# A planned attention-and-MLP kernel: gelu in runs of six, wv loaded among the first x tiles, the last output block in one bank

## The chip, the cores and the metric

The kernel runs on one core of a Trainium2 chip. The metric is device time in microseconds (us). The engines are TensorE (PE in the profile, PEld for its weight loads), VectorE (DVE), ScalarE (ACT), GpSimd (POOL) and SyncE (SP), which here issues every DMA. Each engine runs its own instruction list in order and waits on semaphores for the others.

## What is computed

With x of 2048 rows by 1024, 32 heads of 32, and a hidden width of 3584, all in bf16:

```python
xn = layernorm(x)
s = softmax(q k^T / sqrt(32)) v @ wo            # q, k, v from xn @ wqkv, 32 heads
y = layernorm(xn)
g = silu(gelu(y @ w1 + b1) @ w2 + b2)           # gelu in its tanh form
out = x + s * g
```

## The kernel before

**Tiling.** Attention works in 8 head groups of 4 heads and 8 blocks of 256 queries. A *unit* is one block of queries against 256 keys for the 4 heads of a group: PE computes the scores (line 902, eight matmuls of 256 columns) into two pairs of PSUM banks out of three pairs, ACT takes the exponential of each pair (line 911, 128x1024, two for a unit), and PE multiplies the result with V (line 625). There are 64 units of scores for each head group, so close to a thousand exponentials. VectorE adds the exponentials up for the softmax sums (lines 928 and 942). The MLP works in 8 chunks of 256 rows. A chunk has 14 `w1_item`s; each makes two blocks of 128 hidden units by 256 rows in one bank (line 630) and adds the bias on VectorE into a slot of the ring `hT` of 20 slots (line 1084). Gelu is applied to a *run* of slots that lie side by side: three VectorE instructions (lines 1098 to 1100) prepare the argument in a scratch tile `ut`, ACT takes Tanh (line 1101), and two more VectorE instructions (1102, 1103) finish it in `hT`. Runs have 4 slots (2048 elements a partition) or 2 slots (1024), and use the two `ut` tiles in turn. Then 4 `w2_item`s make the chunk's output (line 630 again), with a Tanh of 1024 elements for the silu (line 1128), and the result goes to DRAM (`g_scratch`). The last head group also does the product with wo and the final `x + s * g` (lines 1428 to 1458).

**The order of the work.** No loop order is fixed by hand. Every instruction is added to a planner (`_Plan`) with its engine, an estimated duration, a priority and the tokens it reads and writes. `run` lays the instructions out in time on all five engines and so decides each engine's order; `settle` turns the dependencies into semaphore waits. PE takes scores first when their inputs are there, then a V group, then "dense" groups (projections, MLP, output) in the order of a position and a due time, each in bank 6 or 7. An instruction once placed waits in its place at run time, and everything behind it on that engine waits too. Durations in the planner steer the order and nothing else.

**The start.** SP issues the loads of x tiles 0 to 3, the first K and Q weights, and x tiles 4 to 11 (`load_x`, line 639). A tile is normalized on VectorE (statistics line 837, result line 796 into `gw`). Tiles 0 to 3 and 5 are transposed on PE (line 780) and copied out by ACT (line 784); the others go through a DMA transpose into `xnT` (line 800, queue of SP). x tiles 12 to 15 and, after tile 13, the first V weights `wv` (line 653) are loaded with a wait for the normalization of tile 4. K of a pair of tiles is projected by `k_item(n)`, its bank copied to SBUF by ACT (line 754) for n below 3 and by VectorE (line 751) from 3 on; Q's bank is copied by VectorE (line 738). The first V groups are `v_half` (line 630, matmuls `ps<-wv,xnT` of 128 columns). Where PE has nothing to do early on, the planner puts in small matmuls on the identity (line 680).

**The end.** The last 256 rows of the output are four blocks of 128x512 (i2 = 0 to 3). For each, the product with wo over head chunks 0 to 6 is finished early in a bank `most`, read by VectorE into an f32 tile (1439) and added to x (1442). The last head chunk, whose input is ready last, goes to another bank (2 to 5); VectorE multiplies it (1452; for block 3 ACT reads the bank, 1447, and VectorE multiplies, 1449), adds the f32 tile (1455, f32 operand) and SP stores the block (1458). The stores carry the tokens `rt` of their row tile, so that the second store of a row tile waits for the first to land.

Of the kernel before, what the change touches and what calls it, by code (L numbers as in the profile page):

```python
# [6 lines left out]
ACT = mybir.ActivationFunctionType  # L7
# [460 lines left out]
def bass_recurrent_scan__mha_block__mixer_channel_mlp__prompt_kernel(  # L468
# [31 lines left out]
    with ExitStack() as st:  # L500
        def sb(name, shape, dt):
            return st.enter_context(nc.sbuf_tensor(name, list(shape), dt))
# [5 lines left out]
        TRP = (5,)  # L508
        PN = ()
        NTR, NWARM, NG0, AT = 4, 8, 3, (1, 3)  # L510
        ident = sb("ident", [128, 128], BF16)
# [16 lines left out]
        b1T = sb("b1T", [128, FB], BF16)  # L528
        ut_t = [sb(f"ut{i}", [128, 4, 512], BF16) for i in range(2)]
        gw = sb("gw", [128, 4096], BF16)  # L530
# [29 lines left out]
        xnb = [gw[:, i * 1024:(i + 1) * 1024] for i in range(4)]  # L560
        iota_i = ut_t[0][:].rearrange("p a b -> p (a b)")[:, 0:256].bitcast(I32)

# [49 lines left out]
        def pool(fn, occ, R, W, prio=3):  # L612
            return add("POOL", fn, occ, PL, R, W, prio)
# [128 lines left out]
        def k_item(n):  # L742
            it = _Item("pro", 0.01 * n)
            for lo, w in ((0, 128), (128, 128)) if n < 2 else ((0, 256),):
                for dc in range(DC):
                    def fn(e, b, dc=dc, lo=lo, w=w):
                        at = n * 256 + lo
                        return mm(e, bank(b, lo, lo + w), wqk[wk0][:, dc, :], xnT[:, dc, at:at + w], dc == 0 and lo == 0, dc == DC - 1)
                    chunk(it, fn, Q256 if w == 256 else Q128, [("xnT", 2 * n + i, dc) for i in range(lo // 128, (lo + w) // 128)] + [("wqk", wk0)])
            if n >= 3:  # L750
                dve(lambda e: e.tensor_copy(QKT[0][:, 1, n * 256:(n + 1) * 256], bank(it.bank, 0, 256)), c_ps(256), [],
                    [("K", 0, n)], -1, it)
                return it
            act(lambda e: e.activation(QKT[0][:, 1, n * 256:(n + 1) * 256], bank(it.bank, 0, 256), ACT.Copy), c_act(256), [],
                [("K", 0, n)], -1, it)
            return it
# [37 lines left out]
        def normalize(t, rs):  # L794
            def nf(e):
                return e.tensor_scalar(xnb[t % 4], xst[t], mv[:, t, 0:1], lnp[:, t, 1:2], op0=ALU.subtract, op1=ALU.mult)  # L796
            rw = ([XS(t), ("mv", t), rs], [("xnb", t % 4)], 1)
            first[t] = pool(nf, 1150, *rw) if t in PN else dve(nf, c_b4(1024) + 118, *rw)
            if t >= NTR and t not in TRP:
                dma(f"tr{t}", lambda e: e.dma_start_transpose(xnT[:, :, t * 128:(t + 1) * 128], xnb[t % 4]), 262144,  # L800
                    [("xnb", t % 4)], [("xnT", t, c) for c in range(DC)], prio=0, rate=300.0, occ=1300, lat={4: 2800, 6: 2400, 7: 2000}.get(t, 1000))

# [260 lines left out]
        def make_y(c):  # L1063
            for t2 in range(2):
# [7 lines left out]
                    262144, [("yst", t2)], [("yT", t2)], occ=1300, rate=300.0, lat=2300)  # L1072

        def w1_item(c, pi):
            p = c * NW1 + pi
            gi, hs = p % NW1R, p % NH
            it = _Item("mlp")
            for f2 in range(2):
# [7 lines left out]
                c_ps(512), [("b1",)], [("h", hs)], 0, it)  # L1086
            half = c == NCH - 1 and pi in (NW1 - 3, NW1 - 1)
            if p % 4 != 3 and pi != NW1 - 1 and not (pi == 1 and c % 2) and not half:
                return it
            k = 2 if (pi == NW1 - 1 and p % 4 != 3) or (pi == 1 and c % 2) or half else 4  # L1090
            h0, n = hs - k + 1, k * 512
            hs_ = [("h", h0 + i) for i in range(k)]
            ui = geg["n"] % 2
            geg["n"] += 1
            x_ = hT[:, h0:h0 + k].rearrange("p s k t -> p (s k t)")
            u_ = ut_t[ui][:].rearrange("p a b -> p (a b)")[:, 0:n]
            gp, ga = (1.4, -1) if c == NCH - 1 and pi >= 5 else (3, 1)
            dve(lambda e: e.tensor_tensor(u_, x_, x_, op=ALU.mult), c_b16(n), hs_, [("ut", ui)], gp)  # L1098
            dve(lambda e: e.tensor_scalar(u_, u_, GA, 1.0, op0=ALU.mult, op1=ALU.add), c_b4(n), [("ut", ui)], [("ut", ui)], gp)
            dve(lambda e: e.tensor_tensor(u_, u_, x_, op=ALU.mult), c_b16(n), [("ut", ui)] + hs_, [("ut", ui)], gp)  # L1100
            act(lambda e: e.activation(u_, u_, ACT.Tanh, scale=GC), c_acts(n), [("ut", ui)], [("ut", ui)], ga)  # L1101
            dve(lambda e: e.tensor_scalar_add(u_, u_, 1.0), c_b4(n), [("ut", ui)], [("ut", ui)], gp)
            dve(lambda e: e.tensor_tensor(x_, u_, x_, op=ALU.mult), c_b16(n), [("ut", ui)] + hs_, hs_, gp)  # L1103
            return it
# [213 lines left out]
        for w in range(HG):  # L1318
# [24 lines left out]
            for qb in range(NQB):  # L1343
# [44 lines left out]
                for t2 in range(2):  # L1388
# [16 lines left out]
                    for nh in range(2):  # L1405
# [3 lines left out]
                        i2 = 2 * t2 + nh  # L1409
                        sl_ = slice(nh * 512, (nh + 1) * 512)  # L1410
                        if late:
                            most = _Item("wo", it.pos + 64)
                            plan.dense["last"].append(most)
                            if fin:
                                it.bank = 2 + 2 * t2 + nh
                                if not t2:
                                    it.due = 64 * HG - 2
                            (plan.dense["wo"] if not fin else lates if t2 else firsts).append(it)
                        for hc in range(HG):
                            def fn(e, b, hc=hc, tb=tb, nh=nh, late=late):  # L1420
                                return mm(e, bank(b), OTr[:, hc, tb * 128:tb * 128 + 128],
                                          wo_at[hc][:, nh * 512:(nh + 1) * 512], hc == 0 or late and hc == HG - 1,
                                          hc == HG - 1 or late and hc == HG - 2)
                            chunk(most if late and hc < HG - 1 else it, fn, Q512,
                                  [("OTr", hc) if hc < 7 else ("OTr", 7, qb) + ((t2,) if fin else ()), ("wo", hc)],
                                  [("S", 1 + t2, nh)] if fin and hc == HG - 1 else ())
                        if not late:
# [9 lines left out]
                        if not fin:  # L1437
                            after([("xf", xk)], [("w1", i) for i in range(NW1R)])
                        dve(lambda e, most=most, gr=gr, sl_=sl_, xf=xf: e.scalar_tensor_tensor(
                            xf, bank(most.bank), 0.5, gr[:, sl_], op0=ALU.mult, op1=ALU.mult),  # L1440
                            c_ps(512), [("gr", ri, nh)], [("xf", xk)] + (zs if fin else []), 0, most)
                        dve(lambda e, xr=xr, sl_=sl_, xf=xf: e.tensor_tensor(xf, xf, xr[:, sl_], op=ALU.add),
                            c_f32(512), [("xr", ri, nh)], [("xf", xk)], 2)
                        if fin and i2 == 3:
# [6 lines left out]
                        else:  # L1451
                            dve(lambda e, it=it, gr=gr, sl_=sl_: e.scalar_tensor_tensor(gr[:, sl_], bank(it.bank), 0.5,
                                                                                        gr[:, sl_], op0=ALU.mult, op1=ALU.mult),
                                c_ps(512), [], [("gr", ri, nh)], -1 if fin and t2 else 0, it)
                        dve(lambda e, xr=xr, gr=gr, sl_=sl_, xf=xf: e.tensor_tensor(xr[:, sl_], gr[:, sl_], xf, op=ALU.add),
                            c_f32(512), [("gr", ri, nh), ("xf", xk)], [("xr", ri, nh)], -1 + 0.1 * i2 if fin and t2 else 2.05 if fin else 1)
                        if fin:
                          dma(f"osl{i2}", lambda e, xr=xr, tb=tb, sl_=sl_: e.dma_start(
                            out2[tb * 128:(tb + 1) * 128, sl_], xr[:, sl_]), 131072, [("xr", ri, nh)], rt, prio=0, rate=390.0, lat=1000.0)
                    if fin:  # L1460
# [69 lines left out]
```

## Time and profile before

| what | value |
|---|---|
| timed runs | 1032.63, 1033.36, 1033.86 us; median 1033.36 |
| the profiled execution | 1032.24 us; its span, from first to last instruction, 1030.3 us |
| busy ACT | 1016.9 us (99%), of it 988 exponentials from line 911 into the tiles P: 922.4 us |
| busy PE, DVE, POOL | 1004.7, 956.3, 11.8 us |
| granted TensorE clock, mean | 0.997 of full speed |

Busy time is the time in which at least one instruction of the engine was running, as the profiler shows it; ends of matmuls are modelled, so PE's figure is not a measure of work at peak. An instruction's duration holds a part in which the next one has already begun, so the distance from start to start is what an instruction costs on a full engine; the chain of waits lists such distances, and the groups list durations.

### The profile page before, as it was taken

The page shows a single profiled execution, that of the slowest core. Times are in us where ns is not written, and L with a number is a line of the kernel's source. Part 1 is how long each engine was busy: PE and PEld are TensorE (multiplying, and loading weights), DVE is VectorE, ACT ScalarE, POOL GpSimd, SP SyncE. Part 2 cuts the span into 40 slices and gives each one's busy share as a digit, 9 for nine tenths or more (in the row PEclk, how much of TensorE's full clock was granted, in tenths as well). Part 3 has the DMA queues.
Part 4 walks back from the last instruction along what each step waited for, and adds up shares of the span by engine and source line. Part 5 has one row for each costly group of instructions (what it writes and reads, how often), then busy time and mean ns, then how long its engine had stood idle before and what let it go on. Part 6 is the DMA issues. An engine that isn't in the chain of part 4 may idle for free.

```text
span 1030.3 us, 31971 instructions
## 1 busy us (share of the span) xinstructions
PE 1004.7 (98%) x14355; PEld 636.6 (62%) x14355; DVE 956.3 (93%) x1347; ACT 1016.9 (99%) x1093; POOL 11.8 (1%) x21
## 2 busy tenths in 40 slices
PE   8999999999999999999999999999999999999996
PEld 6666656666666567566665676666666665654443
DVE  8899999899899999997899989998999889978987
ACT  8999999999999999999999999999999999999996
POOL 2200000000000000000000000000000000000000
PEclk9999999999999999999999999999999999999999
DMA  8867746645765658456547576565455752974321
GB/s 222 158 156 206 200 136 182 170 117 142 204 175 154 182 157 228 125 144 188 139 126 195 143 215 173 158 177 152 118 154 167 216 168 78 279 224 124 112 91 58
DMA packets 317144, 167.75 MB, mean 163 GB/s; under 512 B 55632, under 2 KB 304976, under 8 KB 317008
## 3 DMA queue, kind: packets, MB, share of 16 engines
q1 hardware_dynamic: 317008, 165.71, 58.8%
q8 instruction: 112, 1.84, 0.7%
q14 instruction: 24, 0.20, 0.1%
HBM read 146.55 MB, written 12.06 MB: 154 GB/s over the span
## 4 chain that ended last, share of the span: by engine, by line
ACT 84%; PE 7%; DVE 5%; DMA 2%; issue 0%; SPq 0%; POOL 0%; DVEq 0%
ACT P L911 78%; PE ps L630 4%; ACT ut L1101 4%; PE ps L625 2%; ACT gw L1128 1%; PE ps L902 1%; ACT P L1221 1%; DVE PA L928 1%; DMA wv<-in_A_wqkv_dram 1%; DVE stats L837 1%; DVE PR L942 1%; DVE hT L1084 1%; DMA yst<-in_A_x_dram 1%; DVE gw L796 0%; DMA hT<-in_A_x_dram 0%; DMA xnT<-gw 0%
## 5 line engine op out<-in xcount | busy, mean ns | idle before, releaser
L911 ACT ACTIVATE P<-ps 128x1024 bf16<-128x1024 f32 x988 | 922.4, 1231 | 0.6 <-PE ps L902 0.5
L928 DVE TENSOR_TENSOR PA<-P 128x2048 bf16<-128x2048 bf16 x173 | 209.8, 1215 | 30.0 <-ACT P L911 29.5
L630 PE MATMUL ps<-yT,w1r 128*128 128x256 bf16 x1792 | 228.0, 273 | 0.9 <-DVE V L716 0.4
L630 PE MATMUL ps<-w2r,hT 128*128 128x256 bf16 x1792 | 224.3, 273 | 0.7 <-DVE nt L997 0.3
L942 DVE TENSOR_TENSOR PR<-PR,PA 128x2048 bf16<-128x2048 bf16 x173 | 209.1, 1210 | 1.2
L902 PE MATMUL ps<-QKT 32*128 32x256 bf16 x4032 | 200.4, 273 | 9.2 <-ACT P L911 7.0
L630 PEld LDWEIGHTS ps<-yT,w1r 128*128 128x128 bf16 x1792 | 164.5, 98 | 53.5 <-issue 28.1
L630 PEld LDWEIGHTS ps<-w2r,hT 128*128 128x128 bf16 x1792 | 163.0, 98 | 51.5 <-issue 31.3
L902 PEld LDWEIGHTS ps<-QKT 32*128 32x128 bf16 x4032 | 59.8, 92 | 137.3 <-ACT P L911 129.4
L625 PE MATMUL ps<-P,V 128*32 128x256 bf16 (+1 forms) x4080 | 137.2, 272 | 0.2
L630 PE MATMUL ps<-xnT,wqk 128*128 128x512 bf16 (+2 forms) x584 | 131.3, 354 | 1.1 <-DVE nv L1010 0.3
L625 PEld LDWEIGHTS ps<-P,V 128*32 128x32 bf16 x4080 | 95.6, 96 | 32.7 <-issue 22.6
L630 PE MATMUL ps<-wv,xnT 128*128 128x256 bf16 (+2 forms) x704 | 89.7, 267 | 1.6 <-DMA xnT<-gw 0.6
L630 PEld LDWEIGHTS ps<-xnT,wqk 128*128 128x128 bf16 x584 | 50.0, 98 | 50.7 <-issue 14.4
L1084 DVE TENSOR_TENSOR hT<-ps,b1T 128x512 bf16<-128x512 f32 x112 | 76.6, 684 | 3.7 <-PE ps L630 3.2
L928 DVE TENSOR_TENSOR PR<-P 128x2048 bf16<-128x2048 bf16 x60 | 72.7, 1212 | 0.1
L630 PEld LDWEIGHTS ps<-wv,xnT 128*128 128x128 bf16 x704 | 56.5, 99 | 25.6 <-issue 11.6
L1101 ACT ACTIVATE ut<-ut 128x2048 bf16<-128x2048 bf16 (+1 forms) x33 | 61.4, 1861 | 0.0
L728 DVE CAST QKT<-ps 128x512 bf16<-128x512 f32 x58 | 39.6, 683 | 1.6 <-PE ps L630 1.2
L997 DVE STREAM_TRANSPOSE nt<-ps 128x256 f32<-128x256 f32 x63 | 27.9, 442 | 13.8 <-PE ps L625 13.4
L1103 DVE TENSOR_TENSOR hT<-ut,hT 128x2048 bf16<-128x2048 bf16 (+1 forms) x33 | 34.6, 1049 | 0.1
L1098 DVE TENSOR_TENSOR ut<-hT 128x2048 bf16<-128x2048 bf16 (+1 forms) x33 | 34.7, 1050 | 0.1
(115 smaller groups left out, 584.9 us busy)
## 6 DMA issues: line engine op xcount, KB each, us to landing
w1r<-in_B_w_dram SPq DMA_DIRECT2D x112, 512.0 KB, 4.7
w2r<-in_B_w_dram SPq DMA_DIRECT2D x128, 448.0 KB, 4.5
yst<-in_A_x_dram SPq DMA_DIRECT2D x18, 256.0 KB, 4.7
wqk<-in_A_wqkv_dram SPq DMA_DIRECT2D x16, 256.0 KB, 3.7
g_scratch<-gw SPq DMA_DIRECT2D x32, 128.0 KB, 2.9
hT<-in_A_x_dram SPq DMA_DIRECT2D x14, 256.0 KB, 3.9
o_scratch<-ot SPq DMA_DIRECT2D x56, 64.0 KB, 3.6
xnT<-o_scratch SPq DMA_DIRECT2D x7, 512.0 KB, 5.3
```

Source lines behind the costliest of these rows:

```text
L625: ins = e.matmul(dst(j), lhsT=lhsT(j), rhs=rhs(j), start=start, stop=stop, tile_position=(0, 32 * j), skip_group_check=True)
L630: return e.matmul(dst, lhsT=lhsT, rhs=rhs, start=start, stop=stop, skip_group_check=True)
L728: dve(lambda e: e.tensor_copy(QKT[sl][:, which, tq * 512:(tq + 1) * 512], bank(it.bank)), c_ps(512), [], [(nm, sl, 2 * tq), (nm, sl, 2 * t ...
L902: ins = e.matmul(bank(b0[j], kk * 256, (kk + 1) * 256), lhsT=QKT[sl][32 * j:32 * j + 32, 1, kb * 128:(kb + 1) * 128], rhs=QKT[sl][32 * j:3 ...
L911: x = act(lambda e, h=h: e.activation(Pt[pi][:, 2 * h:2 * h + 2].rearrange("p j k q -> p (j k q)"), ps[:, pr[h] * 1024:(pr[h] + 1) * 1024] ...
L928: return dve(lambda e: e.tensor_tensor(dst[:].rearrange("p u j q -> p (u j) q"), src[:].rearrange("p u j k q -> p (u j) k q")[:, :, 0, :], ...
L942: return dve(lambda e: e.tensor_tensor(fl3(pr), fl3(pr), fl3(PA[i]), op=ALU.add), c_b16(2048), [("PA", i), tok], [tok], 3.2)
L997: dve(lambda e: e.transpose(nt_t[:], bank(pv.bank, 256, 512)), c_ps(256) + 120, [], [("nt",)], prio, pv)
L1084: w1_ev[p] = dve(lambda e: e.tensor_tensor(hT[:, hs], bank(it.bank).rearrange("p (k t) -> p k t", k=2), b1T[:, 2 * pi:2 * pi + 2].unsqueez ...
L1098: dve(lambda e: e.tensor_tensor(u_, x_, x_, op=ALU.mult), c_b16(n), hs_, [("ut", ui)], gp)
L1101: act(lambda e: e.activation(u_, u_, ACT.Tanh, scale=GC), c_acts(n), [("ut", ui)], [("ut", ui)], ga)
L1103: dve(lambda e: e.tensor_tensor(x_, u_, x_, op=ALU.mult), c_b16(n), [("ut", ui)] + hs_, hs_, gp)
```

## The change

Five things change.

1. **Gelu runs.** A table `GRUNS` is made before the MLP: in chunks 0 to 5 a run has up to 6 slots (`GMAX`), in the last two up to 4, never across the end of the ring of 20; in the last chunk it ends in runs of 2. A run of 6 uses both `ut` tiles, now one tensor `utw`, with VectorE's five instructions done in two parts (4 slots and 2 slots) and one Tanh over 3072 elements. The number of runs goes from 33 to 27.
2. **wv and x12 to x15.** `load_v(0)` stands between x9 and x10, with no wait. x12 and x13 are added with a wait for the normalization of tile 4 before pair 3, x14 and x15 with a wait for that of tile 7 before pair 4.
3. **K copy of pair 2** goes from ACT (line 754) to VectorE: `n >= 2`.
4. **The last output block** (i2 = 3) is `whole`: head chunks 0 to 7 add up in one bank, so the f32 copy and its addition (1439, 1442) fall away for this block, ACT still reads the bank, and the last addition has bf16 operands. It stands alone in a queue `pre`.
5. **The final stores** no longer carry `rt`. Some latencies that the planner assumes for DMA transposes change.

```diff
-        for t in range(NTR, 12):
-            load_x(t)
+        load_x(4)
...
+        load_x(9)
+        load_v(0)
+        load_x(10)
+        load_x(11)
...
-            if n >= 3:
+            if n >= 2:
                 dve(lambda e: e.tensor_copy(QKT[0][:, 1, n * 256:(n + 1) * 256], bank(it.bank, 0, 256)), c_ps(256), [],
...
-            if n == 6:
-                for t in range(12, NT):
-                    load_x(t, [first[4]])
-                    if t == 13:
-                        load_v(0, [first[4]])
+            if n == 3:
+                load_x(12, [first[4]])
+                load_x(13, [first[4]])
+            if n == 4:
+                load_x(14, [first[7]])
+                load_x(15, [first[7]])
...
+        GRUNS = {}
+        for c_ in range(NCH):
+            p_, end = c_ * NW1, (c_ + 1) * NW1
+            while p_ < end:
+                k_ = min(GMAX if c_ < 6 else 4, end - p_, NH - p_ % NH)
+                if c_ == NCH - 1:
+                    k_ = min(k_, 2 if end - p_ <= 4 else 4)
+                GRUNS[p_ + k_ - 1] = k_
+                p_ += k_
...
-            act(lambda e: e.activation(u_, u_, ACT.Tanh, scale=GC), c_acts(n), [("ut", ui)], [("ut", ui)], ga)
...
+            for h0, k, ui in parts:
...
+                dve(lambda e, u_=u_, x_=x_: e.tensor_tensor(u_, x_, x_, op=ALU.mult), c_b16(n), hs_, [("ut", ui)], gp)
+                dve(lambda e, u_=u_: e.tensor_scalar(u_, u_, GA, 1.0, op0=ALU.mult, op1=ALU.add), c_b4(n), [("ut", ui)], [("ut", ui)], gp)
+                dve(lambda e, u_=u_, x_=x_: e.tensor_tensor(u_, u_, x_, op=ALU.mult), c_b16(n), [("ut", ui)] + hs_, [("ut", ui)], gp)
...
+            act(lambda e: e.activation(ua, ua, ACT.Tanh, scale=GC), c_acts(run * 512), uts, uts, ga)
...
+                        whole = fin and i2 == 3
...
-                        dve(lambda e, most=most, gr=gr, sl_=sl_, xf=xf: e.scalar_tensor_tensor(
-                            xf, bank(most.bank), 0.5, gr[:, sl_], op0=ALU.mult, op1=ALU.mult),
-                            c_ps(512), [("gr", ri, nh)], [("xf", xk)] + (zs if fin else []), 0, most)
-                        dve(lambda e, xr=xr, sl_=sl_, xf=xf: e.tensor_tensor(xf, xf, xr[:, sl_], op=ALU.add),
-                            c_f32(512), [("xr", ri, nh)], [("xf", xk)], 2)
+                        if not whole:
...
+                        if whole:
+                            dve(lambda e, xr=xr, gr=gr, sl_=sl_: e.tensor_tensor(xr[:, sl_], gr[:, sl_], xr[:, sl_], op=ALU.add),
+                                c_b16(512), [("gr", ri, nh)], [("xr", ri, nh)], -1 + 0.1 * i2)
...
-                            out2[tb * 128:(tb + 1) * 128, sl_], xr[:, sl_]), 131072, [("xr", ri, nh)], rt, prio=0, rate=390.0, lat=1000.0)
+                            out2[tb * 128:(tb + 1) * 128, sl_], xr[:, sl_]), 131072, [("xr", ri, nh)], [], prio=0, rate=390.0, lat=1000.0)
```

More of the change, by code (lines that the diff above doesn't have):

```diff
@@ L509, in bass_recurrent_scan__mha_block__mixer_channel_mlp__prompt_kernel @@
         PN = ()
+        GMAX = 6
         NTR, NWARM, NG0, AT = 4, 8, 3, (1, 3)
@@ L1102, in w1_item @@
-            dve(lambda e: e.tensor_scalar_add(u_, u_, 1.0), c_b4(n), [("ut", ui)], [("ut", ui)], gp)
-            dve(lambda e: e.tensor_tensor(x_, u_, x_, op=ALU.mult), c_b16(n), [("ut", ui)] + hs_, hs_, gp)
+            run = GRUNS.get(p)
+            if run is None:
+                return it
+            hh = hs - run + 1
+            gp, ga = (1.4, -1) if c == NCH - 1 and pi >= 5 else (3, 1)
+            parts = []
+            for h0 in range(hh, hh + run, 4):
+                k = min(4, hh + run - h0)
+                ui = 0 if h0 > hh or run > 4 else geg["n"] % 2
+                parts.append([h0, k, ui])
@@ new lines, in w1_item @@
+            if run > 4:
+                parts[1][2] = 1
+                geg["n"] = 0
+            else:
+                geg["n"] += 1
+            views = []
+            for h0, k, ui in parts:
+                hs_ = [("h", h0 + i) for i in range(k)]
+                n = k * 512
+                x_ = hT[:, h0:h0 + k].rearrange("p s k t -> p (s k t)")
+                u_ = utw[:, 4 * ui:4 * ui + k].rearrange("p a b -> p (a b)")
+                views.append((x_, u_, n, hs_, ui))
+                dve(lambda e, u_=u_, x_=x_: e.tensor_tensor(u_, x_, x_, op=ALU.mult), c_b16(n), hs_, [("ut", ui)], gp)
+                dve(lambda e, u_=u_: e.tensor_scalar(u_, u_, GA, 1.0, op0=ALU.mult, op1=ALU.add), c_b4(n), [("ut", ui)], [("ut", ui)], gp)
+                dve(lambda e, u_=u_, x_=x_: e.tensor_tensor(u_, u_, x_, op=ALU.mult), c_b16(n), [("ut", ui)] + hs_, [("ut", ui)], gp)
@@ new lines, in w1_item @@
+            u0 = 4 * parts[0][2]
+            ua = utw[:, u0:u0 + run].rearrange("p a b -> p (a b)")
+            uts = [("ut", q_[2]) for q_ in parts]
+            act(lambda e: e.activation(ua, ua, ACT.Tanh, scale=GC), c_acts(run * 512), uts, uts, ga)
+            for x_, u_, n, hs_, ui in views:
+                dve(lambda e, u_=u_: e.tensor_scalar_add(u_, u_, 1.0), c_b4(n), [("ut", ui)], [("ut", ui)], gp)
+                dve(lambda e, u_=u_, x_=x_: e.tensor_tensor(x_, u_, x_, op=ALU.mult), c_b16(n), [("ut", ui)] + hs_, hs_, gp)
```

53 lines of the change are left out of this document (28 added, 25 removed).

## The prediction

> **What bounds the kernel now.** I read the page's busy times and chain of waits first, then ACT alone in order of time, since it is the fullest engine.
>
> ```profile
> PE 1004.7 (98%) x14355; PEld 636.6 (62%) x14355; DVE 956.3 (93%) x1347; ACT 1016.9 (99%) x1093; POOL 11.8 (1%) x21
> ...
> ACT 84%; PE 7%; DVE 5%; DMA 2%; issue 0%; SPq 0%; POOL 0%; DVEq 0%
> ```
>
> ACT is busy 1016.9 of 1030.3 us. Its idle time is only 13.4 us, and the busy times by stretch place it: 3.36 us in 0 to 20 us, 1.81 in 20 to 40, 0.42 in 40 to 60, 0.03 in 60 to 1000, and 7.76 in the last 30.3, where after the last exponential (1021.94) the other engines finish alone. So a change gains three ways only: less work on ACT, less idle ACT at the start, a shorter end. Anything on PE, DVE or DMA in between is worth nothing unless it makes ACT wait.
>
> ACT at the start, in order of time (start, length, line; idle time before and its releaser in brackets):
>
> ```profile
> 17.09 4.75 ACT L911 ACTIVATE P<-ps 128x1024 bf16<-128x1024 f32 x5
> 21.61 0.51 ACT L754 ACTIVATE QKT<-ps 128x256 bf16<-128x256 f32 x1
> 22.62 3.77 ACT L911 ACTIVATE P<-ps 128x1024 bf16<-128x1024 f32 x4 [0.51 <-PE ps L902]
> 27.46 1.94 ACT L911 ACTIVATE V<-ps 128x1024 bf16<-128x1024 f32 x2 [1.06 <-PE ps L902]
> 29.64 1.94 ACT L911 ACTIVATE QKT<-ps 128x1024 bf16<-128x1024 f32 x2 [0.24 <-PE ps L902]
> ```
>
> The K copy of pair 2 (L754) sits behind five exponentials; the scores of unit 4 need it, so ACT then idles 0.51 us. The idle 1.06 and 0.24 us come before units 6 and 7. A last 0.39 us comes at 44.41 (unit 15). PE in the same time says why:
>
> ```profile
> 19.83 1.91 PE L630 MATMUL ps<-xnT,wqk 128*128 128x256 bf16 x16
> 22.18 0.40 PE L902 MATMUL ps<-QKT 32*128 32x256 bf16 x8 [0.43 <-ACT QKT L754]
> 22.50 0.40 PE L680 MATMUL ps<-ident 128*128 128x128 bf16 x4
> 23.70 0.40 PE L902 MATMUL ps<-QKT 32*128 32x256 bf16 x8 [0.80 <-ACT P L911]
> 24.45 2.41 PE L630 MATMUL ps<-wv,xnT 128*128 128x128 bf16 x25 [0.35 <-DMA wv<-in_A_wqkv_dram]
> 26.79 0.61 PE L902 MATMUL ps<-QKT 32*128 32x256 bf16 x8
> ```
>
> Unit 6's scores (26.79) stand behind 25 V matmuls that waited for wv, and these ran at 2.41/25 = 96 ns; at 29.52, 22 of them took 1.40 us, 64 ns. The stretches show the granted clock (column after POOL):
>
> ```profile
> 21.50:25.00 3.50, 1.92 (x33) 1.02 (x31) 3.50 (x9) 3.00 (x5) 0.48 (x1) 1.00 1.43 189
> 25.00:28.40 3.40, 3.40 (x36) 2.73 (x34) 1.91 (x6) 2.33 (x4) 0.70 (x1) 0.50 0.91 204
> 28.40:31.80 3.40, 3.40 (x57) 2.60 (x56) 3.10 (x7) 3.16 (x5) 0.00 (x0) 1.00 0.43 97
> ```
>
> After 3.5 us with PE 55% busy the clock was halved for 3.4 us. An earlier stretch (14.70 to 18.10) with PE 83% busy was followed by full clock. **The rule on the clock.** The Trainium skill, page "TensorE: Matmul & The Clock Gate", section "What's actually happening", gives a free-running activity window of 3413 ns and half rate after an idle one; the 3.4 us agree, but the window before it was not idle, so the trace puts the threshold higher than the page does. By the page alone a repeat after the change would depend on where its windows happen to fall.
>
> **The start after the change.** The changed order of instructions keeps PE's, ACT's and DVE's lists up to 19.6 us.
> - wv moves ahead of x10 and x11 in SP's queue, so these two issue 0.43 us later and their bytes follow half a megabyte. wv took 6.98 us to land amid 1 MB of x; issued near 8.9 us it is there by about 16, needed at 23.5. x10 is first read near 21.4; the slowest x landing is 7.2 us after issue, so it is there too. The transpose of tile 4 (issued 14.95) may meet the tail of this: nothing if it lands by 20.06; its landing is unseen, the transposes' median is 3.0 and longest 6.1 us, so 0 to 1 us late; I take 0, as the median leaves 2 us.
> - Of the old group of five loads at 16.35, x12 and x13 stay, wv goes, and x14 and x15 go behind the transposes of tiles 6 to 9. Those of 6 and 7 took 2.45 us to issue then, others 1.31; with a third of the bytes ahead I expect 1.31. x14 then issues near 25.9 and lands by 29 to 33 (2.9 to 7.2 us); VectorE reads it near 31, with 1.4 us of slack to the unit that needs it.
> - K copy: four more identity matmuls (0.06 us each from start to start) put K and Q of pair 2 at 20.06. K's 8 matmuls (0.119 each) end at 21.0. VectorE, in order, is free at 21.1; the copy takes 0.41 us (L738's row). The scores of unit 4 stand behind 13 matmuls: 20.06 + 13 x 0.119 = 21.61 instead of 22.18, and the exponentials come 0.44 later as before: 22.05, not 22.62. ACT's other work is done at 21.61.
> - Unit 5: scores after the first exponential of unit 4, 23.13 (1.08 after, as before), exponentials at 23.88. wv being there, the 25 V matmuls follow at 23.46 and take 1.60 us at 64 ns. Unit 6's scores run at 25.06, ended before ACT is free at 25.70. Then 7 V matmuls (0.45) and K of pair 3 (0.95) leave unit 7's scores at 26.8, needed by 27.2. Unit 7 starts at 27.53 instead of 29.64: **2.1 us**.
> - VectorE, which idled 1.49 us before the V copy at 28.30, normalizes tiles 10 to 15 some 2 us earlier, so their transposes follow. Unit 15's wait, behind the transpose of tile 15 (39.38 + 4.54), has moved on PE behind unit 15; unit 16 needs it at 43.7 and gets it near 43.3. I count 0.3 of 0.39. Start: **-2.4 us**; bounds 0 and -2.6.
>
> **Gelu.** Rows by form:
>
> ```profile
> L1101 ACT ACTIVATE ut<-ut 128x2048 bf16<-128x2048 bf16 x23 | 48.6, 2113 | 0.0
> L1101 ACT ACTIVATE ut<-ut 128x1024 bf16<-128x1024 bf16 x10 | 12.8, 1281 | 0.0
> ```
>
> In the chain of waits, where ACT is full, a Tanh costs 1.79 (2048) and 0.94 us (1024): 0.85 a thousand elements and 0.085 fixed. A Tanh of 3072 is not in the trace: 1.79 + 0.85 = 2.64. Elements are unchanged, six Tanhs fall away: 6 x 0.085 = **-0.5 us**. VectorE gets 37 parts instead of 33; splitting a part costs 3 x (2 x 0.677 - 1.213) + 2 x (2 x 0.408 - 0.677) = 0.70 us, so +2.8 us, hidden in VectorE's 59 us idle between 60 and 1000 (6.8 us of 200 in its fullest stretch, 500 to 700).
>
> **The end.** VectorE, then SP's last two stores:
>
> ```profile
> 1023.92 0.68 DVE L1455 TENSOR_TENSOR hT<-hT,gw 128x512 bf16<-128x512 bf16 x1
> 1024.52 0.68 DVE L1452 SCALAR_TENSOR_TENSOR hT<-ps,hT 128x512 bf16<-128x512 f32 x1
> 1025.23 0.69 DVE L1455 TENSOR_TENSOR hT<-hT,gw 128x512 bf16<-128x512 bf16 x1
> 1025.84 0.42 DVE L1449 TENSOR_TENSOR hT<-hT,PR 128x512 bf16<-128x512 bf16 x1
> 1026.29 1.29 DVE L1455 TENSOR_TENSOR hT<-hT,gw 128x512 bf16<-128x512 bf16 x2
> ```
> ```profile
> 1027.61 0.81 SPq L1458 DMA_DIRECT2D out_dram<-hT  x2
> ```
>
> Before, two of the additions for blocks 0 and 1 stood at 1023.92 and 1026.98; the last store issued at 1027.97 behind block 1's. Now L1439 and L1442 of block 3 go, and both additions stand ahead of the transpose at 1022.80. The multiplications start at 1020.69 (PE's end 1020.65); four steps of 0.60 end at 1023.10, so the transpose is 0.30 late, and with it PE's last matmuls (1024.36). Block 2: 1024.79, addition 1025.50, block 3's product 1026.11, its addition 1026.56, now 0.42 as the bf16 form of L1431 (417 ns): 1026.98, store 1027.01. **-1.0 us**. The dropped waits on `rt` held nothing here: the third store issued 0.03 us after VectorE.
>
> **Sum.** -2.4 - 0.5 - 1.0 = -3.9 us on the profiled 1032.24: 1028.3. That execution lies 1.1 us below the median of the runs; set on the median, 1033.36 - 3.9 = **1029.5**.
>
> **Rivals.**
> - *Half clock again* (17%): PE still waits about 0.75 us before unit 5, so a stretch may be only some 75% busy, between the 55% that lost the clock and the 83% that kept it. At 96 ns the V matmuls end at 25.87, unit 6's exponentials start at 26.5 (0.8 lost), unit 7's 0.4 later still: -2.7 in all, 1030.7.
> - *The lead is given back* (17%): x14, x15 or a transpose lands late (7.2 and 6.1 us were seen), and before 60 us ACT waits as long as it had gained. Only end and Tanh remain: 1031.9. Against it: VectorE and SP run ahead too.
> - *Slower* (7%): a run of six ends its gelu 3.3 us later than one of four (Tanh 0.85, and the second part's 3 x 0.60 + 2 x 0.34). If a w2 group on PE waits for it, scores queue behind and ACT starves. There are 10 such runs; a single exposed wait eats 3.3 of the 3.9, and from two on it is slower: three give 1039. Against it: 0.03 us of ACT idle with 33 runs before, and the second runs are short.
> - *More than forecast* (7%): below 1028.2, were the profiled time typical.
>
> The forecast has 52%. The range 1028.2 to 1032.4 holds the forecast and the first two rivals. A measurement tells about 0.2% (2.07 us) from no change: faster holds the forecast, the clock rival and the low case, 76%; same the third case, 17%; slower 7%.
>
> **What would show it.** Right: unit 7 (into QKT) at about 27.5; full clock from 25.0 to 28.4; no wait of PE for wv; 27 Tanhs; idle ACT near 0 from 60 to 1000; last store about 5.1 us after the last exponential's end, not 6.0. Wrong: ACT waiting in 60 to 1000, VectorE waiting for x14, or a half-clock stretch.

## The result, and the profile after

The changed kernel takes 1031.03 us (median of 14 runs, 1029.88 to 1033.99) against 1033.0 (14 runs, 1032.11 to 1034.54): ratio 0.9984, interval 0.9976 to 0.9992, so 0.8 to 2.5 us less, where 3.9 were forecast. Each ratio here is against the kernel before, run beside it, and is worked out over all runs, so that it differs a little from the quotient of the medians; brackets behind it hold a 95% interval. In a second comparison, among the experiments, it is 0.9990 (0.9981 to 0.9999). The time lies inside the range, 1.5 us above the forecast of 1029.5. The profiled execution took 1032.43 us, 0.2 more than the profiled one of before, although each step of the change is in it. That makes it worth reading, since whatever ate 3.9 us must show.

First the busy line and the chain, from the page of after:

```profile
PE 1004.1 (97%) x14355; PEld 637.2 (62%) x14355; DVE 956.3 (93%) x1366; ACT 1016.4 (99%) x1086; POOL 12.4 (1%) x21
...
ACT 84%; PE 7%; DVE 5%; DMA 2%; issue 1%; POOL 0%; SPq 0%
```

ACT is 0.5 us less busy, and "issue" in the chain went from 0 to 1%: for part of the span an engine waited for nothing that the profile names. At the start ACT does what was forecast (start, length; idle before in brackets):

```profile
22.41 3.77 ACT L921 ACTIVATE P<-ps 128x1024 bf16<-128x1024 f32 x4 [0.22 <-PE ps L912]
26.04 1.98 ACT L921 ACTIVATE V<-ps 128x1024 bf16<-128x1024 f32 x2
27.84 2.00 ACT L921 ACTIVATE QKT<-ps 128x1024 bf16<-128x1024 f32 x2
```

Unit 7 (into QKT) starts at 27.84, not 29.64; the first exponentials are 0.33 us later in this execution, so the step is 2.13 us. The lead is gone 30 us later. ACT in order of time:

```profile
55.96 1.94 ACT L921 ACTIVATE P<-ps 128x1024 bf16<-128x1024 f32 x2 [2.00 <-PE ps L912]
59.04 3.77 ACT L921 ACTIVATE P<-ps 128x1024 bf16<-128x1024 f32 x4 [1.14 <-PE ps L912]
```

Together 3.14 us idle, against 0.42 in the whole stretch 40 to 60 before. PE in the same time:

```profile
51.73 0.40 PE L627 MATMUL ps<-P,V 128*32 128x256 bf16 x8
54.01 1.06 PE L627 MATMUL ps<-P,V 128*32 128x256 bf16 x32 [1.88 <-issue]
54.89 0.47 PE L627 MATMUL ps<-w1r,V 128*32 128x256 bf16 x8
```

Forty matmuls of one group belong together; PE stopped after eight for 1.88 us, and the releaser is "issue". Only the first of the forty waits on a semaphore. The stretches (busy of PE, PEld, DVE, ACT, POOL; clock; DMA share, GB/s) show the second half of the damage, a clock halved behind the gap:

```profile
52.10:54.10 2.00, 0.12 (x8) 0.10 (x8) 2.00 (x5) 1.86 (x3) 0.00 (x0) 1.00 1.04 108
...
55.20:58.20 3.00, 3.00 (x32) 1.03 (x28) 0.66 (x2) 1.94 (x2) 0.00 (x0) 0.50 1.08 296
```

The end is as forecast. VectorE's last two steps, the second now a bf16 addition:

```profile
1027.38 0.42 DVE L1490 TENSOR_TENSOR hT<-hT,PR 128x512 bf16<-128x512 bf16 x1
1027.83 0.42 DVE L1497 TENSOR_TENSOR hT<-hT 128x512 bf16<-128x512 bf16 x1
```

The last exponential ends at 1023.23, the span at 1030.6: 7.37 us, where before it was 1021.94 to 1030.3, 8.36.

**Theory 1**, formed on this: PE's instructions are streamed, and a late packet of them stopped PE. The queue table of the page has a row for them:

```profile
q8 instruction: 113, 1.85, 0.8%
```

113 packets of 16.4 KB for 28,710 matmuls and weight loads: one packet for 254 of these, about 127 matmuls. With the 189 other instructions that the trace has on PE's list it is 256. The stall stands at PE's 731st matmul. The kernel before has one of 0.41 us, hidden, at its 859th: 128 later. One packet starts after each 128th of these matmuls, in the median 0.7 us after it from 80 us on, and in this stretch late: the 603rd started at 47.7, the packet at 51.5, and PE went on at 54.01. From 44 to 60 us the DMA engines are full (share 0.94 to 1.23): the load of b2 (256 KB, 7.4 us to land), a wqk load and the transposes into yT. Rivals: the stall belongs to that instruction or the order of the matmuls; or to the gelu runs or the end.

### The profile page after: what moved, and what is told of

Its sections match the earlier page's. It is cut to its first block, busy times and chain, and to the rows that moved or that the text cites. A ratio compares the mean times of both kernels' runs of the same rounds, so it can differ in the third digit from the quotient of the medians.

```text
span 1030.6 us, 31984 instructions
## 1 busy us (share of the span) xinstructions
PE 1004.1 (97%) x14355; PEld 637.2 (62%) x14355; DVE 956.3 (93%) x1366; ACT 1016.4 (99%) x1086; POOL 12.4 (1%) x21
## 4 chain that ended last, share of the span: by engine, by line
ACT 84%; PE 7%; DVE 5%; DMA 2%; issue 1%; POOL 0%; SPq 0%
ACT P L921 78%; PE ps L632 5%; ACT ut L1135 4%; DVE stats L847 1%; PE ps L627 1%; PE ps L912 1%; ACT gw L1163 1%; ACT P L1256 1%; DMA w2r<-in_B_w_dram 1%; DVE gw L805 1%; DVE PA L938 1%; DMA xnT<-gw 0%; DMA hT<-in_A_x_dram 0%; DVE PR L952 0%; DVE ut L1129 0%
## 5 line engine op out<-in xcount | busy, mean ns | idle before, releaser
L632 PEld LDWEIGHTS ps<-yT,w1r 128*128 128x128 bf16 x1792 | 164.3, 98 | 52.9 <-issue 29.6
L632 PEld LDWEIGHTS ps<-w2r,hT 128*128 128x128 bf16 x1792 | 163.1, 98 | 53.4 <-issue 30.2
L632 PEld LDWEIGHTS ps<-xnT,wqk 128*128 128x128 bf16 x584 | 50.0, 98 | 50.1 <-issue 16.4
L1135 ACT ACTIVATE ut<-ut 128x3072 bf16<-128x3072 bf16 (+2 forms) x27 | 59.3, 2197 | 0.0
```

Of the source, the lines that this page charges most:

```text
L632: return e.matmul(dst, lhsT=lhsT, rhs=rhs, start=start, stop=stop, skip_group_check=True)
L1135: act(lambda e: e.activation(ua, ua, ACT.Tanh, scale=GC), c_acts(run * 512), uts, uts, ga)
```

## The experiments

**Moving the suspected bytes.**

```diff
+        b2_ = [o for o in sp_ if o.sem == "b2"][0]
+        to_ = [o for o in sp_ if o.sem.startswith("w1") and o.sem[2:].isdigit()][3]
+        for l_ in (sp_, sq_):
+            l_.remove(b2_)
+            l_.insert(l_.index(to_) + 1, b2_)
```

> The changed kernel with one DMA moved: the load that broadcasts b2 (half a megabyte written into SBUF) goes behind the fourth w1 load in SyncE's list; every other instruction stays in its place. Theory 1 (TensorE's instructions, fetched in packets of 16 KB over the same DMA engines, came late because the engines were full from 44 to 60 us): the stall of 1.88 us inside the 40 P,V matmuls at 52.1 us is gone or under 0.3 us, ACT's idle time from 40 to 60 us falls from 3.32 to 0.5 us or less, a run takes about 3 us less than the profiled run of the changed kernel (1029.5 against 1032.43), and no run lies near 1033: median about 1029.9, 3.1 us below the kernel before. Rival A (the stall belongs to that instruction or to the order of the matmuls): it stays at the same matmul with 1.9 us, ACT idles 3.3 us again, and the time is that of the changed kernel. Rival B (the stall is there but the runs above 1032 come from something else): the stall goes, and runs near 1033 remain.

(The load is 256 KB, not half a megabyte.) Measured: 1029.98 us against 1032.33, ratio 0.9977 (0.9968 to 0.9987), 9 runs from 1028.63 to 1031.09. The packet starts at 50.2, no stall is listed, ACT is not idle from 40 to 60 us:

```profile
52.08 1.51 PE L627 MATMUL ps<-P,V 128*32 128x256 bf16 x40
```

But 2.35 us is not 3.1: ACT idles 0.61 us at 33.4, and 0.97 between 60 and 1000. How full the engines are is not what counts: from 48 to 52 us their share is 1.57 here against 1.23 in the changed kernel, and yet the packet starts 1.2 us earlier. Which transfer holds it up was not traced.

**The changed kernel again.** No edit.

> The changed kernel, unchanged, beside the others. The 14 runs so far lie in two groups, 1029.9 to 1031.1 (8 or 9 of them) and 1031.9 to 1034.0. Theory 1 (late instruction packets, a race between two streams of DMA, so now in time and now not): two groups again, and the profile shows either a stall of 1 to 2 us at a matmul whose number is 91 more than a multiple of 128 and about 3 us of idle ACT in 40 to 60 us (a run near 1032.5), or no stall and idle ACT under 0.8 us (a run near 1030). Rival (the stall is in every run): all profiles show 3.3 us of idle ACT, whatever the time. Median 1031, 2 us below the kernel before.

Measured: 1031.49, ratio 0.9990. The profiled run has the stall at the same matmul, 1.48 us, and loses 1.31 us of ACT by it; no half clock followed. The 11 times do not fall in two groups (1030.25 to 1031.97 without a gap, one at 1033.89), so that part of theory 1 falls: in these two profiles the stall varies in length rather than being there or not. Against this run the kernel with b2 moved is 1.5 us faster by the medians.

**The start alone.** The kernel before with parts 2 and 3.

```diff
+        load_v(0)
...
-            if n >= 3:
+            if n >= 2:
...
+            if n == 4:
+                load_x(14, [first[7]])
```

> The kernel before with the loads and the K copy of the change alone (parts 2 and 3); gelu and the end as before. By the terms of the prediction: the first exponential into QKT starts 2.1 us earlier (27.5 against 29.6), clock at full speed from 25.0 to 28.4, -2.4 us in all. Theory 1: TensorE then reaches its 731st matmul 1.8 us earlier, while its next packet of instructions has not come, so in the runs where the packet is late (the profile shows it by the stall) 2 to 3.1 us of ACT are lost at 52 to 59 us: median -0.5 to -2 us against the kernel before, single runs -2.4 or +0.7. Rival (the stall comes from the gelu runs of six or from the end): no stall, every run 2.4 us faster.

Measured: 1032.33 against 1032.33, ratio 1.0003 (0.9995 to 1.0012). Unit 7 is early as in the changed kernel, and the stall is there, at the same matmul, with gelu and the end as before:

```profile
54.12 1.06 PE L625 MATMUL ps<-P,V 128*32 128x256 bf16 x32 [1.18 <-issue]
```

So the stall comes from the start, and **the start as it stands gains nothing that these runs can tell**. ACT loses 0.92 us at 33.6 and 1.01 at 54.8.

**Moving the boundary.** The changed kernel, its identity matmuls split in two.

```diff
-            for _ in range(n):
+            for _ in range(n if n == 1 else 2 * n):
+                w_ = 128 if n == 1 else 64
```

> The changed kernel with its small matmuls on the identity (after the first 6 us) issued as twice as many of half the width: the same TensorE time within about 2 us spread over waits, 76 matmuls more, so that the 256-instruction boundaries fall on other matmuls. Theory 1: a stall, where there is one, stands at a matmul whose number in this kernel's own count is 91 more than a multiple of 128, so no longer behind the first 8 of the 40 P,V matmuls, but 76 matmuls earlier in the program; its length may be anything from 0 to 3 us, since the packet is then asked for earlier, near 44 us. Rival A (the stall belongs to that instruction or that wait): it stands behind the first 8 of the same 40 P,V matmuls, 1.9 us.

Measured: 1030.54, ratio 0.9982 (0.9973 to 0.9990). The forty P,V matmuls now run in one piece, with no stall anywhere near:

```profile
52.76 1.28 PE L627 MATMUL ps<-P,V 128*32 128x256 bf16 x40
```

The 603rd matmul of this kernel's own count comes at 43.0, and its packet started at 42.8. The rival, a stall that belongs to the instruction, is out. ACT idles 1.24 us at 35 us, more than in any other profile, and that needs a reason of its own (it stands below, behind theory 3).

**Theory 2**, on that wait. After's profile has only 0.15 us there, the four profiles just told 0.91 to 1.46 us of PE, for the transpose of tile 10 (in the last one of tile 11; the expectations say 11 throughout). In the kernel with b2 moved:

```profile
31.07 1.07 PE L632 MATMUL ps<-wv,xnT 128*128 128x128 bf16 x16
33.04 0.62 PE L632 MATMUL ps<-wv,xnT 128*128 128x128 bf16 x8 [0.91 <-DMA xnT<-gw]
```

Is the transpose issued too late, or does it land too slowly? First, earlier issue:

```diff
+        vc_, mv_ = dv_[i_ - 1], dv_[i_ + 1:j_]
+        mv_ = [mv_[1], mv_[0]] + mv_[2:]
+        for l_ in (dv_, sq_):
+            l_.remove(vc_)
+            l_.insert(l_.index(mk[10]) + 1, vc_)
...
+            k_ = l_.index(first[11]) + 1
+            l_[k_:k_] = mv_
```

> The kernel with b2's load moved, and on VectorE the normalizations of x tiles 10 and 11 now ahead of a copy of V's bank's successors: the order is 1/sqrt's argument, V copy, the two normalizations, K copy, statistics of tile 12 (before: V copy, argument, statistics of tile 12, K copy, normalizations). Theory 2 (the other part of the lost lead is the transpose of tile 11, which waits for its normalization and lands about 0.9 us after TensorE wants it): the normalizations start near 27.1 instead of 27.88 us, TensorE's wait for the transposed tile at 33 us falls from 0.91 to 0.3 us or less, ACT's idle 0.61 us at 33.4 us goes, and the median is 0.5 us below that of the kernel with b2 moved alone (2.35 us below before there), so about 2.9 us below the kernel before. Rival (the transpose is bound by the DMA queue or the engines, not by when it is issued): the wait stays near 0.9 us, and the time is that of the kernel with b2 moved.

Measured: ratio 0.9976 (0.9965 to 0.9987), the same as without it. The normalizations start at 27.38 and the first transpose issues at 27.95, half a microsecond earlier, but the two take 5.8 and 5.3 us to land instead of 4.6 and 4.1, and PE waits 1.36 us. Theory 2 falls for its rival: to issue them half a microsecond earlier gains nothing. What lies ahead of them is x14 and x15, issued at 26.38 here.

**Controls on the kernel before.** Its b2 load moved in the same way; the new end alone (parts 4 and 5); gelu in runs of six alone (part 1).

```diff
+        b2_ = [o for o in sp_ if o.sem == "b2"][0]
...
+            l_.insert(l_.index(to_) + 1, b2_)
```

> The kernel before, with the load of b2 moved behind the fourth w1 load and nothing else. Theory 1 (the late packet of instructions costs only where TensorE has got ahead of it, and the kernel before, 1.8 us later at that matmul, waits 0.41 us that other idle time covers): no difference, within 0.4 us of the kernel before. Rival (moving b2 is worth something by itself, whatever the start): about 1.5 us less here too, as between the changed kernel (1031.49) and the one with b2 moved (1029.98).

Measured: 0.9995 (0.9984 to 1.0007). Moving b2 by itself does nothing that can be told: as far as these runs show, it is worth something only to a kernel that comes early.

```diff
+                        whole = fin and i2 == 3
...
-                            out2[tb * 128:(tb + 1) * 128, sl_], xr[:, sl_]), 131072, [("xr", ri, nh)], rt, prio=0, rate=390.0, lat=1000.0)
+                            out2[tb * 128:(tb + 1) * 128, sl_], xr[:, sl_]), 131072, [("xr", ri, nh)], [], prio=0, rate=390.0, lat=1000.0)
```

> The kernel before with the last block in one bank and the stores without their wait (parts 4 and 5) alone. By the prediction: the span ends 7.4 us after the last exponential has ended instead of 8.4, -1.0 us in all, and the start and ACT's idle time up to 1000 us stay as they were. Rival (a shorter end is taken up by the last store's landing or by VectorE's order): 8.4 us again, no difference.

Measured: 0.9991 (0.9982 to 1.0001), about -0.9 us, though the interval just reaches no change. After 1000 us ACT is idle 6.67 us, against 7.76 before; every kernel here with the old end has 7.75 to 7.79, every one with the new end 6.62 to 6.95. The expectation "the start stays as it was" missed, in a way that helps: this execution came through the *old* start without waiting for wv, with unit 7 at 28.22, and ran into the same packet:

```profile
53.40 1.06 PE L625 MATMUL ps<-P,V 128*32 128x256 bf16 x32 [0.82 <-issue]
```

```diff
+                k_ = min(GMAX if c_ < 6 else 4, end - p_, NH - p_ % NH)
...
+            act(lambda e: e.activation(ua, ua, ACT.Tanh, scale=GC), c_acts(run * 512), uts, uts, ga)
```

> The kernel before with gelu in runs of six (part 1) alone: 27 Tanhs instead of 33. By the prediction: -0.5 us (six times 0.085), ACT's busy time 0.5 us lower, no wait of TensorE for gelu. Rival (runs of six make w2 groups wait, 3.3 us for each exposed one, or bring their weights late): ACT idle 0.5 us or more between 60 and 1000 us, and no gain or a loss.

Measured: 0.9998 (0.9990 to 1.0007), which holds -0.5 us and holds none. ACT is busy 1016.59 us, against 1016.92 before and 1016.80 to 1017.34 in the other kernels with the old gelu and the K copy on ACT; it idles 0.23 us between 60 and 1000. No wait for gelu.

**Theory 3**, on the transposes: the bytes of x14 and x15 ahead of them. The base is run again on the same chip.

```diff
-                load_x(14, [first[7]])
-                load_x(15, [first[7]])
+                load_x(14, [first[4]])
+                load_x(15, [first[4]])
```

> The kernel with b2's load moved, unchanged, as the base for the next two on the same chip: 2.3 us below the kernel before (0.9977 of it), ACT idle 0.5 to 1.2 us at 33 to 35 us behind the transpose of tile 11 and no stall at 52 us.

> The kernel with b2's load moved, and the loads of x tiles 14 and 15 right behind those of 12 and 13 (near 17.6 us) instead of behind the transposes of tiles 6 to 9 (26.3 us); nothing else moves. Theory 3 (the transposes of tiles 10 and 11, issued at 28.4 and 29.7, take 3.9 to 5.8 us to land because half a megabyte of x14 and x15 lies ahead of them on the DMA engines, and 2.8 where nothing does): they land within 3.2 us, TensorE does not wait for them at 33 us (0.9 to 1.4 us now), ACT's idle time near 34 us goes, and the median is 0.6 us below the same kernel with the loads late. Against it could go: the transposes of tiles 6 and 7, at 21 us, meet the earlier bytes (in the kernel before they took 2.45 us to issue and 4.5 to land), and TensorE's K matmuls of pair 3 near 26 us wait for them, 0.5 to 0.8 us, so that nothing is gained. Rival (the transposes of 10 and 11 are slow by their place among TensorE's or VectorE's traffic): they take 4 to 5 us as before, and the time is unchanged.

Measured: the base 0.9981 (0.9970 to 0.9993), with a stall of 0.62 us at the 731st matmul this time (the packet at 50.4), so moving b2 shortens the stall and doesn't rule it out. Two of its twelve runs lie above 1033 (1033.32 and 1034.63), so rival B of the first test, slow runs that come from something else, is not out. With x14 and x15 early 1029.41 (5 runs), **ratio 0.9969** (0.9957 to 0.9981), 2.0 to 4.4 us less than before: the best version by its ratio, and clear of the kernel before. Over its base it gains 1.6 us by the medians, but the two intervals overlap; the wait in the traces tells more. Only SyncE's order differs from its base. From the views of the transfers, the transpose of tile 10 (issue to landing, in the kernel with b2 moved, then with x14 early):

```profile
xnT<-gw SPq DMA_TRANSPOSE x1, 4.6
```
```profile
xnT<-gw SPq DMA_TRANSPOSE x1, 2.8
```

And PE in the second one, without the wait at 33 us:

```profile
30.97 1.51 PE L632 MATMUL ps<-wv,xnT 128*128 128x128 bf16 x24
32.81 0.62 PE L632 MATMUL ps<-wv,xnT 128*128 128x128 bf16 x8
```

ACT's idle time from 20 to 40 us is 0.22 us, that before unit 4 and no other. The objection, transposes of tiles 6 and 7 against the earlier bytes, shows (4.0 and 3.5 us to land) and costs nothing.

That the order of the loads costs the wait is shown; that it is their bytes alone is not, for the edit moves something else. PE's packet of instructions in this stretch starts at 28.30 us with x14 and x15 early, as tile 10's transpose is issued (28.32), and at 29.5 to 30.2 in the six profiles with the loads late and the identity matmuls whole, while that transpose is under way. Two profiles part the two causes. In the kernel with wv alone (told below) no x load is ahead, and between 29.1 and 29.3 us the only packet on the DMA engines is that of the instructions; tile 10's transpose, issued at 28.52, is still late:

```profile
q8 instruction: 1, 0.02, 41.7%
...
xnT<-gw SPq DMA_TRANSPOSE x1, 3.8
```

In the kernel with the boundary moved the packet starts at 32.44 instead. There tile 10, behind the bytes alone, takes 3.9 us and PE waits 0.17 for it; tile 11, with the packet in it, takes 5.0, and PE waits 1.46 for it. So the long wait has moved with the packet, and it is what ACT's 1.24 us at 35 us come from. By these traces theory 3 told half of the cause: bytes ahead and a packet of instructions each go with a late transpose, and late loads bring the two together. No run was made to separate them, so how much each is worth stays open.

> The last kernel with the normalizations of tiles 10 and 11 ahead as well (0.5 us earlier, which alone gained nothing). Theory 3: with no bytes ahead of them, the transposes now land 0.5 us earlier too, so that a remaining wait of TensorE at 33 us goes; median equal to the last kernel where no wait is left there, else up to 0.5 us less. If theory 1 is right, the lead may again run into the instruction packet at 52 us: a stall of 0 to 0.5 us there.

The edit is the one of theory 2 on top. Measured: 0.9974 (0.9964 to 0.9984), no gain over the last; with nothing left to wait for at 33 us, nothing was to be had. The stall at the packet at 50.5 us is 0.41 us.

**wv alone.** The kernel before with wv's load moved between x9 and x10, and x12 to x15 together as before.

```diff
+        load_v(0)
+        load_x(10)
+        load_x(11)
...
-                    if t == 13:
-                        load_v(0, [first[4]])
```

> The kernel before with wv's load alone moved between those of x9 and x10 (x12 to x15 as before, K copy of pair 2 on ScalarE). By the prediction's steps: no wait of TensorE for wv (0.35 us before), the V matmuls at 64 ns and not 96, full clock from 25.0 to 28.4, and the exponentials into QKT (unit 7) start about 1.5 us earlier, near 28.1 instead of 29.64; of that at most 0.5 us is left at the end, since theory 1 caps the lead at the packet of instructions near 52 us. Rival (the clock, not wv, held unit 7): half clock again from 25.0, unit 7 less than 0.6 us earlier.

Measured: 0.9988 (0.9979 to 0.9997), about -1.2 us, where at most 0.5 was expected. Unit 7 starts at 28.26, the V matmuls run at 64 ns, the clock is full. Its lead over the old start is kept, since it meets the packet just in time (50.4, no stall). It does stall 0.68 us at the next packet, at its 859th matmul, but ACT has work in hand and idles nowhere from 52.75 to 64.9 us. One line of the change did better alone than all of its start (1.0003), though the two intervals just touch and the runs were on different chips.

**The packet in all profiles.** Times in us, of every profile in which the boundary stands at the same matmul: the start of the 603rd matmul, of the next packet and of the 732nd matmul, with which the last 32 of the forty begin.

| kernel | 603rd | packet | 732nd | stall |
|---|---|---|---|---|
| after | 47.7 | 51.5 | 54.0 | 1.88 |
| after again | 48.2 | 51.2 | 54.0 | 1.48 |
| start alone | 48.6 | 51.7 | 54.1 | 1.18 |
| end alone | 47.9 | 51.0 | 53.4 | 0.82 |
| b2 moved, again | 47.9 | 50.4 | 52.9 | 0.62 |
| x14 early | 47.3 | 49.8 | 52.3 | 0.62 |
| x14 early, normalizations early | 48.1 | 50.5 | 52.9 | 0.41 |
| b2 moved | 48.1 | 50.2 | 52.5 | none listed |
| b2 moved, normalizations early | 48.8 | 50.9 | 53.2 | none listed |
| wv alone | 48.2 | 50.4 | 52.8 | none listed |
| gelu alone | 49.0 | 51.3 | 53.7 | none listed |
| before | 49.3 | 51.6 | 54.1 | none listed |
| before, b2 moved | 49.7 | 51.1 | 54.2 | none listed |

In the seven with a stall PE goes on 2.4 to 2.85 us after the packet's start, whatever the length of the stall. Five of the six without one get there 2.3 to 2.5 us after it, so they have next to no reserve; only the kernel before with b2 moved has, at 3.0 us.

## Why the prediction was right or wrong

**Right: the schedule of the start.** From the third-last exponential ahead of the K copy (at 18.90 before) to unit 7 the forecast was 27.53 - 18.90 = 8.63 us; after, after again, the start alone, b2 moved and x14 early all have 8.60. Full clock, wv not waited for, K copy off ACT: as listed.

**Wrong: the size of that step against what it replaces.** These 2.1 us were set against one execution of the old start. The same distance in four profiles of the old start is 10.74 (before), 10.37 (b2 moved in it), 9.91 (gelu alone) and 9.30 (end alone): mean 10.08, so the step is 1.5 us on average, and 2.1 was the far end.

**Wrong: "so their transposes follow"**, and zero for x14 and x15 behind the transposes of tiles 6 to 9. In six profiles with the loads of x14 and x15 there the transposes of 10 and 11 came late and cost ACT 0.61 to 1.24 us; only after's first profile escaped. The rival *the lead is given back* named this case ("x14, x15 or a transpose lands late") and put 17% on it.

**Wrong: nothing was counted for instructions.** The same rival's end, ACT waiting before 60 us as long as it had gained, came in after's profile by a second way that the text did not name: 3.14 us behind the packet, 1.31 and 1.01 in the next two profiles. This is the larger part there. So the term -2.4, with bounds 0 and -2.6, measured +0.3 us (-0.5 to 1.2), by the start alone. For after's own execution: -2.13 - 0.5 (Tanh, as forecast) - 0.99 + 0.33 (first exponentials later) + 3.14 = -0.15, where the difference measured was +0.2. The rival's price for the whole, 1031.9, is 0.9 us from the median 1031.03, the forecast 1.5 us. So the step that failed is the start, the largest term of the sum; that the time still lies in the range is due to the range, which was drawn to hold this rival, and not to the forecast's mechanism. Two of the signs that the prediction gave for being wrong came: a half-clock stretch, and ACT waiting in 60 to 1000 us (0.33 us in after, 1.21 in after again). VectorE did not wait for x14 in after.

The Trainium skill, page "Runtime: NRT & Kernel Launch", section "Instruction fetch mechanics", gives blocks of 256 instructions that each engine fetches by a DMA queue of its own, and calls the cost of a crossing mostly hidden. The packet size agrees (254 matmuls and weight loads, 256 with the others). That the cost is hidden holds for the rest of this kernel (no other stall with "issue" of 0.4 us or more from 60 to 1000 us in after), and fails where 128 matmuls pass in 4.1 us (603rd to 731st) and the packet between them starts 3.7 us late.

**Right: the end**, -1.0 forecast, -0.99 in the traces, 0.9991 by time (its interval reaches 1.0001). **Right in form: gelu.** The chain of waits of after has the Tanh of a run of six at the 2.64 us that were worked out; there are 10 of these among 27 Tanhs:

```profile
131.45 2.64 ACT ut L1135
```

The 0.5 us lie below what the runs can tell. The rival of w2 groups waiting for runs of six is not seen with gelu alone.

**Right: the reading of the clock** (55% busy lost it, 83% kept it), once it is redone on the clock's own windows. The clock record of before changes at 4.49, 24.97 and 28.39 us, that of after at 7.28, 55.07 and 58.48, all close to whole multiples of 3.413 us apart. If each profile is cut so from its first change, these windows have PE least busy (after, before, after again, the kernel with the boundary moved):

```profile
51.66:55.07 3.41, 1.53 (x56) 1.09 (x48) 3.41 (x8) 2.30 (x3) 0.00 (x0) 1.00 1.30 141
21.56:24.97 3.41, 1.83 (x32) 0.99 (x31) 3.41 (x9) 2.90 (x5) 0.42 (x1) 1.00 1.45 187
51.05:54.46 3.41, 1.93 (x64) 1.21 (x60) 3.38 (x7) 3.35 (x4) 0.00 (x0) 1.00 1.10 140
31.98:35.39 3.41, 1.78 (x29) 1.29 (x28) 2.14 (x6) 3.20 (x4) 0.07 (x1) 1.00 0.53 120
```

Half clock followed the first two, with PE 45 and 54% busy, and no other window up to 1000 us in any profile. The third, 57% busy, kept the clock, and so did the fourth at 52%, the one case out of order; its identity matmuls are cut in two. The Trainium skill, page "TensorE: Matmul & The Clock Gate", section "What's actually happening", has half rate follow a free-running window that was idle. The grid agrees with that; but the windows that lost the clock here were about half busy, so the prediction's sentence that the trace puts the threshold higher stands. What it lacked is that a stretch cut by hand is not one of the windows.

**Still open.** Between 60 and 1000 us ACT idles 0.03 to 0.77 us in the five profiles with the old start or wv alone, and 0.13 to 2.18 in the nine with the new start. PE mostly waits there for w2 loads, 0.2 to 1.1 us at a time, near 198, 615 and 914 us. With the transposes it can account for what b2 moved falls short of 3.1 us; why the loads come late was not tried. The waits for w2 near 198 and 615 us stand in the eight profiles that have both runs of six and the new start (each has one or both), and in none of the six others, so that the two together bring w2 late is a rival that no run tests. Nor was it tried how often a run has the long stall with the half clock behind it.

## What to carry to other kernels

A lead on the fullest engine is kept only if every stream behind it can follow: count the transfers, and count the instructions of the engine that runs ahead, which are a transfer too and can hold up others. A stall inside a group that shares one wait, with "issue" as its releaser, at a distance of 128 matmuls from another, is the sign; moving a transfer out of the time before it (1.5 us here), or the boundary itself (0.95 us), helps, but a moved boundary can hit another transfer, as the transpose of tile 11 shows. And a wait that is to be removed should be measured on several executions, since one profile may show its far end.

## What the runs showed of the hardware

- A packet of PE's instructions (16.4 KB) holds 256 of them. In after it started 0.4 to 2.9 us after the crossing of 128 matmuls up to 40 us, 3.7 us after it at 47.7 us, and 0.7 us in the median from 80 us on. In none of the 14 profiles did PE pass a crossing less than 2.3 us after the start of the packet that followed the crossing before, so the traces show no more than one packet fetched ahead.
- A window of 3.41 us with PE 45% (after) or 54% busy (before) was followed by 3.4 us at half clock; windows of 57% and more were not, nor was one of 52%.
- The transpose of a tile lands 2.7 to 2.8 us after issue with nothing ahead and no packet of instructions in it, 3.9 us with two x loads (512 KB) issued 1.0 to 1.6 us before it (the kernel with the boundary moved), 3.0, 3.3 and 3.8 us with a packet of instructions alone (before; x14 early with the normalizations early; wv alone), and that of tile 10 3.8 to 5.8 us with both.
